# Masked copies of two batches merged over four PSUM banks, with a new order of the first four steps

## The chip, the cores and the metric

The kernel runs on one core of a Trainium2 chip. The metric is the device time of one execution in microseconds. TensorE (PE) multiplies matrices, with its weight loads shown apart (PEld); VectorE (DVE) and ScalarE (ACT) work element by element; GpSimd (POOL) and SyncE (SP) mostly issue transfers here.

## The reference

Two blocks follow each other: a gated linear attention over a state, and a two-layer network with a PReLU between its layers.

```python
# q, k, v, f_logit: (4 batches, 8 heads, 768 tokens, 48)
f = 1.0 / (1.0 + np.exp(-f_logit))
for t in range(S):
    state = f[:, :, t, :, None] * state + np.einsum('bhd,bhe->bhde', k[:, :, t], v[:, :, t])
    y[:, :, t] = np.einsum('bhd,bhde->bhe', q[:, :, t], state)

x = y.transpose(0, 2, 1, 3).reshape(3072, 384)
h = x @ w_in                                     # 384 -> 2048
g = np.maximum(h, 0.0) + alpha * np.minimum(h, 0.0)
out = g @ w_out                                  # 2048 -> 384
```

## The kernel before

The tokens of a batch are cut into 6 chunks of 128, and batches are taken in pairs (`U = 2`). That makes 12 steps: step n is a chunk `c` of a pair `bp`, `steps = [(bp, c) for c in range(NC) for bp in range(B // U)]`, so steps 0 and 1 are the first chunks of both pairs (c = 0), steps 2 and 3 the second, and so on. Each step has seven generators, whose stages end at a `yield`:

- **P** (`prepare`, 8 stages): loads q, k, f and v; sigmoid of f on ACT; products of the gates on DVE; copies of queries into the matrix `A` on ACT (L454, the last stage). It makes `qd`, `k4` and `us`, scaled queries and keys, and for c = 0 `k16` and `q16` in its fifth stage.
- **S** and **T** (`scores`, 4 stages each): the scores inside blocks of 32 tokens, S for the pair's first batch (u = 0) and T for its second (u = 1). Stage 1 is 32 small products of `k` and `qd` into PSUM (L580), stage 2 four masked copies out of PSUM into `ad` (L589, one for each lag d), stage 3 32 products of `k4` and `us` into the same banks, stage 4 masked copies again (seven of L599, or three of L615 where c = 0).
- **O** (`carry`): scores between blocks (L512), copied into `A` by ACT (L519), and the products that carry the state on (L543), added to `vs` by DVE (L553, L557). For c = 0 it has extra stages: products of `k16` and `q16` (L490), transposes (L529) and their copies by ACT (L533, one for each batch). It has 8 stages for c = 0 and 4 otherwise.
- **Y** (`attend`): ACT copies `ad` into `A` (L623, two stages of two copies), PE multiplies `A` by `vs` (L634), ACT copies the result out (L641), DVE updates `vs`, and y is transposed into `xT` by transfers, or in step 0 by products (L653).
- **K**, **M**: transposed keys for c > 0, by transfers.
- **n** (`network`): eight stages of products by `w_in` (L679), with the PReLU by ACT (L684) and DVE (L686), and then products by `w_out` (L718, or L699 in step 0).

Four single letters prepare the weights: **a**/**w** for `w_in` (ACT, then DVE L248) and **b**/**g** for `w_out`; each `a` and `b` also issues a load on SP into one of three raw buffers. **W** makes sums of `w_out`, **X** frees the banks of `more` for the network, **i** is one product of ones that nothing reads (L790), **j** 16 pairs of small ones (L798).

PSUM has eight banks of 512 f32 numbers per partition. Two tiles `pair0` and `pair1` have two banks each:

```python
pairs = [psa.tile([128, 2, 512], F32, tag=f"pair{n}", name=f"pair{n}") for n in range(2)]
```

`scores` writes `pairs[u]`; `carry` writes `off = home[0]` with L512 and `home[1]` with L490, L529 and L543; `attend` writes `pairs[0]` with L634. In step 0 `carry` and `attend` use `more` instead. The network has four further banks in turn.

The order in which PE, DVE, ACT and SP get their instructions is written out by hand as a list of stages: `START` for the first steps, then `USUAL` once a step, from step 5 on (`BEGUN = 5`). A letter with a number names the generator of that step, a letter with `+` in `USUAL` that of the next step, `n` that of the step before, and `:4` repeats. Each engine works through its own part of this list in order. POOL's order isn't written out; the scheduler sets it.

Of the kernel before, what the change touches and what calls it, by code (L numbers as in the profile page):

```python
# [8 lines left out]
F32 = mybir.dt.float32  # L9
# [3 lines left out]
I32 = mybir.dt.int32  # L13
# [5 lines left out]
DB = 32  # L19
MASKED = (1, 0)  # L20

U = 2
CH = 64
NC2 = C // CH
NB = DB // 4
# [3 lines left out]

BEGUN = 5  # L30
START = (
# [7 lines left out]
)  # L39
USUAL = "T:2 S:2 n:4 M T:2 S n P+ S n P+ n:3 Y O P+ O:2 Y O n P+ Y:2 P+ n:3 P+:3 K+"  # L40

LOOSE = ("a", "w", "b", "g", "W", "i", "j", "X")

def flat(start, usual, steps=12):
    out = []
    for word in start.split():
        key, _, times = word.partition(":")
        out += [(key,) if key in LOOSE else (key[0], int(key[1:]))] * int(times or 1)
    for n in range(BEGUN, steps + 1):
        for word in usual.split():  # L50
            key, _, times = word.partition(":")
            m = n + key.count("+") - (key == "n")
            if m < steps:
                out += [(key[0], m)] * int(times or 1)
    return out

ORDER = flat(START, USUAL)


@with_exitstack  # L60
def kernel(
# [31 lines left out]
    B, NC, _, HP, _ = qT.shape  # L93
    DM = v.shape[-1]
    H = 2 * HP
# [4 lines left out]
    T = U * C  # L100
    W = U * HP * C
# [7 lines left out]
    UW = UO.pop()  # L109
    VO = [0, 0, DB, DB + 16]  # L110
    VW = DB + 24
    QO = [0]
# [8 lines left out]
    psa = ctx.enter_context(tc.tile_pool(name="psa", bufs=1, space=bass.MemoryType.PSUM))  # L121
    early_ps = ExitStack()
    psb = early_ps.enter_context(tc.tile_pool(name="psb", bufs=1, space=bass.MemoryType.PSUM))
    pairs = [psa.tile([128, 2, 512], F32, tag=f"pair{n}", name=f"pair{n}") for n in range(2)]
    more = [psb.tile([128, 2, 512], F32, tag=f"more{n}", name=f"more{n}") for n in range(2)]
    net = {}

# [35 lines left out]
    mraw = const.tile([128, 4, NB, 4], F32, tag="mraw", name="mraw")  # L163
# [6 lines left out]
    mquad = const.tile([128, UW], F32, tag="mquad", name="mquad")  # L170
    nc.gpsimd.memset(mquad, 0.0)
    for m in range(1, NB):
        lo = UO[m] + (4 if m == 1 else 0)
        n = NB - m
        nc.gpsimd.tensor_copy(mquad[:, lo:lo + 4 * n].rearrange("p (i r) -> p i r", r=4),
                              inq[:, 0:n].unsqueeze(2).broadcast_to((128, n, 4)))
    mhalf = const.tile([128, VW], F32, tag="mhalf", name="mhalf")
    nc.gpsimd.memset(mhalf, 0.0)
    for half in range(2):
        for m in range(1, NQ):  # L180
            n = NQ - m
            lo = 16 * half + 4 if m == 1 else VO[m] + 4 * n * half
            nc.gpsimd.tensor_copy(mhalf[:, lo:lo + 4 * n].rearrange("p (i r) -> p i r", r=4),  # L183
                                  inq[:, NQ * half:NQ * half + n].unsqueeze(2).broadcast_to((128, n, 4)))
    ad = const.tile([128, U, 2, HP, DB], F32, tag="ad", name="ad")
# [76 lines left out]
    def rows(par):  # L262
        return slice(64 * par, 64 * par + D)
# [302 lines left out]
    def scores(u, bp, c, x):  # L566

        k = x["k"]


        QL, QS = (UW, UW) if c else (VW, C)
        to = pairs[u]

        def products(keys, by, lo, hi, step):
            for hp in range(HP):
                for j in range(NJ):
                    g = (u * HP + hp) * NJ + j
                    for par in range(2):
                        r_ = rows(par)
                        nc.tensor.matmul(to[DB * j:DB * (j + 1), par, hp * step + lo:hp * step + hi],  # L580
                                         lhsT=keys[r_, g * DB:(g + 1) * DB], rhs=by[r_, g, lo:hi], start=True, stop=True)

        products(k, qd, 0, QW, C)
        yield
        adu = ad[:, u].rearrange("p r h (i t) -> p (r h) i t", t=4)
        rv = to.rearrange("p r (h x) -> p (r h) x", h=HP)
        for d in range(4):
            n = 4 - d
            nc.vector.copy_predicated(  # L589
                adu[:, :, :, d:4], mraw[:, d, :, d:4].bitcast(I32).unsqueeze(1).broadcast_to((128, H, NB, n)),  # L590
                rv[:, :, QO[d]:QO[d] + NB * n].rearrange("p h (i t) -> p h i t", t=n))
        yield
        products(x["k4"], x["us"], 4, QL, QS)
        yield
        if c:
            for m in range(1, NB):
                lo = UO[m] + (4 if m == 1 else 0)
                n = DB - 4 * m
                nc.vector.copy_predicated(  # L599
                    ad[:, u, :, :, 4 * m:DB],  # L600
                    mquad[:, lo:lo + n].bitcast(I32).unsqueeze(1).unsqueeze(1).broadcast_to((128, 2, HP, n)),
                    to[:, :, 0:HP * UW].rearrange("p r (h x) -> p r h x", h=HP)[:, :, :, lo:lo + n])
        else:
            qv = to.rearrange("p r (h x) -> p (r h) x", h=HP)
            adh = ad[:, u].rearrange("p r h (a t) -> p (r h) a t", a=2)
            for m in range(1, NQ):
                n = 4 * (NQ - m)
                lo = 4 if m == 1 else VO[m]
                hi = lo + (DB - 4 if m == 1 else 2 * n)
                then, of, by = ad[:, u].rearrange("p r h t -> p (r h) t")[:, :, 4:DB], qv[:, :, lo:hi], mhalf[:, lo:hi]  # L610
                by = by.bitcast(I32).unsqueeze(1).broadcast_to((128, H, hi - lo))
                if m > 1:
                    then = adh[:, :, :, 4 * m:16]
                    of, by = (t.rearrange("p h (a t) -> p h a t", a=2) for t in (of, by))
                nc.vector.copy_predicated(then, by, of)  # L615
        yield
# [193 lines left out]
    with tc.manual_schedule(engines={mybir.EngineType.PE, mybir.EngineType.DVE, mybir.EngineType.Activation,  # L810
                                     mybir.EngineType.SP}):
        run = {}
        for n, step in enumerate(steps):
            x = {}
            for key, stage_ in zip("POYKMn", (prepare, carry, attend, keys_moved, landed, network)):
                run[key, n] = stage_(*step, x)
            run["S", n], run["T", n] = (scores(u, *step, x) for u in range(U))
        for key in ORDER:
            next(run[key] if key in run else pieces[key[0]])
# [55 lines left out]
```

## Time and profile before

| | us |
|---|---|
| median of 3 runs (lowest, highest) | 602.37 (602.04, 604.54) |
| the profiled execution | 602.81 |
| its span, first to last instruction | 601.0 |
| PE busy, PEld busy | 575.6, 516.8 |
| DVE busy (998 instructions) | 494.7 |
| ACT busy | 247.4 |
| POOL busy | 85.4 |

Busy times are sums over one engine and overlap with those of the others. L12 is line 12 of the kernel before. A PE product in f32 shows as two instructions, so 32 products are a group of x64. In a line of the timeline stand the start, the time that the group took, engine, line, operation, what is written from what, the shape, the count, and in brackets how long the engine sat idle before and what ended that. TensorE's granted clock was 0.999 over the span.

### The profile page before, as it was taken

The page shows a single profiled execution, that of the slowest core. Times are in us where ns is not written, and L with a number is a line of the kernel's source. Part 1 is how long each engine was busy: PE and PEld are TensorE (multiplying, and loading weights), DVE is VectorE, ACT ScalarE, POOL GpSimd, SP SyncE. Part 2 cuts the span into 40 slices and gives each one's busy share as a digit, 9 for nine tenths or more (in the row PEclk, how much of TensorE's full clock was granted, in tenths as well). Part 3 has the DMA queues.
Part 4 walks back from the last instruction along what each step waited for, and adds up shares of the span by engine and source line. Part 5 has one row for each costly group of instructions (what it writes and reads, how often), then busy time and mean ns, then how long its engine had stood idle before and what let it go on. Part 6 is the DMA issues. An engine that isn't in the chain of part 4 may idle for free.

```text
span 601.0 us, 18092 instructions
## 1 busy us (share of the span) xinstructions
PE 575.6 (96%) x7760; PEld 516.8 (86%) x7760; DVE 494.7 (82%) x998; ACT 247.4 (41%) x430; POOL 85.4 (14%) x162
## 2 busy tenths in 40 slices
PE   2489999999999999999999999999999999999997
PEld 1378667898899899899899899899899899899997
DVE  7989998997888779988988988988988987882351
ACT  5679952621461450550461451452343344232110
POOL 9210014013002103001200300300300300300000
PEclk9999999999999999999999999999999999999999
DMA  8778736015005302502601601601601511201000
GB/s 263 254 216 295 249 89 125 1 48 130 2 2 161 52 1 59 156 1 56 157 2 55 159 3 56 158 2 41 170 4 30 155 31 27 55 1 29 27 1 27
DMA packets 52880, 50.36 MB, mean 84 GB/s; under 512 B 26720, under 2 KB 43360, under 8 KB 52800
## 3 DMA queue, kind: packets, MB, share of 16 engines
q1 hardware_dynamic: 42784, 37.46, 21.7%
q0 software_dynamic: 5504, 9.90, 6.7%
q10 hardware_dynamic: 4512, 1.85, 1.3%
q8 instruction: 61, 1.00, 0.7%
q14 instruction: 19, 0.16, 0.1%
HBM read 36.21 MB, written 4.72 MB: 68 GB/s over the span
## 4 chain that ended last, share of the span: by engine, by line
PE 88%; DVE 7%; ACT 2%; POOL 1%; issue 1%; DMA 0%; DVEq 0%; ACTq 0%; POOLq 0%
PE ph L679 40%; PE pa L718 10%; PE pc L718 10%; PE pair L580 6%; PE pe L718 5%; PE pd L718 5%; PE pb L718 5%; PE pair L634 3%; PE pair L543 1%; DVE w_out_sb L248 1%; PE pair L512 1%; PE po L699 1%; DVE gate L686 1%; POOL mhalf L183 1%; DMA f<-in_fT 0%
## 5 line engine op out<-in xcount | busy, mean ns | idle before, releaser
L679 PE MATMUL ph<-xT,w_in_sb 128*128 128x256 f32 x1152 | 255.3, 381 | 1.4 <-DVE w_in_sb L248 1.4
L679 PEld LDWEIGHTS ph<-xT,w_in_sb 128*128 128x128 f32 x1152 | 216.9, 190 | 33.4 <-issue 2.4
L686 DVE SCALAR_TENSOR_TENSOR gate<-neg,om,ph 128x256 f32<-128x256 f32 x192 | 81.2, 476 | 33.0 <-ACT neg L684 33.0
L684 ACT ACTIVATE neg<-ph 128x512 f32<-128x512 f32 x96 | 56.1, 594 | 121.2 <-PE ph L679 101.6
L718 PE MATMUL pa<-w_out_sb,gate 128*128 128x192 f32 x352 | 62.1, 330 | 0.0
L718 PE MATMUL pc<-t,S 128*128 128x192 f32 x352 | 61.6, 328 | 0.0
L454 ACT COPY A<-q 48x512 f32<-48x512 f32 x44 | 27.1, 617 | 83.4 <-DVE q L408 82.9
L718 PEld LDWEIGHTS pa<-w_out_sb,gate 128*128 128x128 f32 x352 | 57.4, 190 | 1.3
L464 POOL DMA_DIRECT2D ksn<-kt x80 | 46.2, 586 | 85.9 <-DVE kt L422 61.3
L718 PEld LDWEIGHTS pc<-t,S 128*128 128x128 f32 x352 | 57.4, 190 | 0.4
L664 POOL DMA_DIRECT2D xT<-y x22 | 11.9, 544 | 287.5 <-ACT y L641 287.4
L599 DVE COPY_PREDICATED ad<-mquad,pair 128x224 f32<-128x224 int32 (+6 forms) x140 | 41.7, 299 | 4.1
L589 DVE COPY_PREDICATED ad<-mraw,pair 128x256 f32<-128x256 int32 (+1 forms) x96 | 41.2, 451 | 4.0 <-PE pair L580 0.8
L364 DVE TENSOR_TENSOR us<-us,fs 128x768 f32<-128x768 f32 (+5 forms) x60 | 36.9, 615 | 1.1
L765 DVE TENSOR_TENSOR S<-gate 128x512 f32<-128x512 f32 x44 | 30.3, 688 | 0.8
L718 PE MATMUL pe<-w_out_sb,S 128*128 128x192 f32 x176 | 30.6, 327 | 0.0
L718 PE MATMUL pb<-t,gate 128*128 128x192 f32 x176 | 30.4, 326 | 0.0
L718 PE MATMUL pd<-w_out_sb,S 128*128 128x192 f32 x176 | 30.4, 326 | 0.0
L623 ACT COPY A<-ad 32x512 f32<-32x512 f32 x48 | 29.4, 613 | 0.6
L641 ACT COPY y<-pair 128x512 f32<-128x512 f32 x22 | 11.8, 589 | 43.4 <-PE pair L634 43.4
L718 PEld LDWEIGHTS pe<-w_out_sb,S 128*128 128x128 f32 x176 | 28.8, 190 | 0.2
L718 PEld LDWEIGHTS pb<-t,gate 128*128 128x128 f32 x176 | 28.9, 190 | 0.0
(125 smaller groups left out, 710.6 us busy)
## 6 DMA issues: line engine op xcount, KB each, us to landing
w_out_raw<-in_w_out SPq DMA_DIRECT2D x8, 767.8 KB, 7.9
w_in_raw<-in_w_in SPq DMA_DIRECT2D x8, 767.2 KB, 9.5
out<-o SPq DMA_DIRECT2D x23, 192.0 KB, 1.9
q<-in_qT SPq DMA_DIRECT2D x8, 512.0 KB, 4.6
k<-in_kT SPq DMA_DIRECT2D x8, 512.0 KB, 7.1
f<-in_fT SPq DMA_DIRECT2D x7, 512.0 KB, 3.9
vs<-in_v SPq DMA_DIRECT2D x16, 192.0 KB
ksn<-kt SPq DMA_DIRECT2D x80, 32.0 KB, 2.2
```

Of the source, the lines that this page charges most:

```text
L364: nc.vector.tensor_tensor(us[:, :, UO[m]:UO[m] + 4 * n].rearrange("p g (i r) -> p g i r", r=4), us[:, :, skip:skip + 4 * n].rearrange("p g ...
L454: nc.scalar.copy(A[halves(cc)[1], :, par * HP:(par + 1) * HP, CH * cc:CH * (cc + 1)], q3[rows(par)].rearrange("p (u h c) s t -> p u h c (s ...
L464: (nc.gpsimd if a % 2 else nc.sync).dma_start(out=ksn[32 * b:32 * (b + 1)].rearrange("p u (h x) -> p (u h) x", h=HP)[:, :, 32 * a:32 * a + n],
L580: nc.tensor.matmul(to[DB * j:DB * (j + 1), par, hp * step + lo:hp * step + hi], lhsT=keys[r_, g * DB:(g + 1) * DB], rhs=by[r_, g, lo:hi], ...
L589: nc.vector.copy_predicated(adu[:, :, :, d:4], mraw[:, d, :, d:4].bitcast(I32).unsqueeze(1).broadcast_to((128, H, NB, n)), rv[:, :, QO[d]: ...
L599: nc.vector.copy_predicated(ad[:, u, :, :, 4 * m:DB], mquad[:, lo:lo + n].bitcast(I32).unsqueeze(1).unsqueeze(1).broadcast_to((128, 2, HP, ...
L623: nc.scalar.copy(A[s_].rearrange("p u h t -> p (u h) t")[:, :, s_], ad[s_].rearrange("p u r h t -> p (u r h) t"))
L679: nc.tensor.matmul(ph[:, j * T:(j + 1) * T], lhsT=w_in_sb[:, kt, m * 128:(m + 1) * 128], rhs=xT[:, kt], start=(kt == 0 and j == 0), stop=( ...
L684: nc.scalar.activation(neg, phv, AF.Relu, scale=-1.0)
L686: nc.vector.scalar_tensor_tensor(gate[:, m % NH, m // NH], neg[:, j], om[:, m:m + 1], phv[:, j], ALU.mult, ALU.add)
L718: nc.tensor.matmul(to[:, 0:DH], lhsT=of(f), rhs=by(f), start=(f == 0 and not more), stop=(f == NH - 1), skip_group_check=True)
L765: nc.vector.tensor_tensor(to, x_, y_, op)
```

## The change

The copies of stage 2 and stage 4 are taken out of S and made once, in T, for both batches: each instruction then reads all four banks, and there are 4 and 7 (or 3) of them for a step in place of 8 and 14 (or 6). For that the two tiles become one of four banks, with `pairs[0]` and `pairs[1]` as views of it. S's stages 2 and 4 are left empty.

```diff
-    pairs = [psa.tile([128, 2, 512], F32, tag=f"pair{n}", name=f"pair{n}") for n in range(2)]
+    four = psa.tile([128, 4, 512], F32, tag="pair", name="pair")
+    pairs = [four[:, 2 * n:2 * n + 2] for n in range(2)]
...
         products(k, qd, 0, QW, C)
         yield
-        adu = ad[:, u].rearrange("p r h (i t) -> p (r h) i t", t=4)
-        rv = to.rearrange("p r (h x) -> p (r h) x", h=HP)
-        for d in range(4):
+        for d in range(4 if u else 0):
             n = 4 - d
             nc.vector.copy_predicated(
-                adu[:, :, :, d:4], mraw[:, d, :, d:4].bitcast(I32).unsqueeze(1).broadcast_to((128, H, NB, n)),
-                rv[:, :, QO[d]:QO[d] + NB * n].rearrange("p h (i t) -> p h i t", t=n))
+                ad.rearrange("p u r h (i t) -> p (u r h) i t", t=4)[:, :, :, d:4],
+                mraw[:, d, :, d:4].bitcast(I32).unsqueeze(1).broadcast_to((128, U * H, NB, n)),
+                four.rearrange("p b (h x) -> p (b h) x", h=HP)[:, :, QO[d]:QO[d] + NB * n].rearrange("p h (i t) -> p h i t", t=n))
         yield
         products(x["k4"], x["us"], 4, QL, QS)
         yield
-        if c:
+        if not u:
+            pass
+        elif c:
             for m in range(1, NB):
                 lo = UO[m] + (4 if m == 1 else 0)
                 n = DB - 4 * m
                 nc.vector.copy_predicated(
-                    ad[:, u, :, :, 4 * m:DB],
-                    mquad[:, lo:lo + n].bitcast(I32).unsqueeze(1).unsqueeze(1).broadcast_to((128, 2, HP, n)),
-                    to[:, :, 0:HP * UW].rearrange("p r (h x) -> p r h x", h=HP)[:, :, :, lo:lo + n])
+                    ad.rearrange("p u r h t -> p (u r) h t")[:, :, :, 4 * m:DB],
+                    mquad[:, lo:lo + n].bitcast(I32).unsqueeze(1).unsqueeze(1).broadcast_to((128, 2 * U, HP, n)),
+                    four[:, :, 0:HP * UW].rearrange("p b (h x) -> p b h x", h=HP)[:, :, :, lo:lo + n])
         else:
...
```

The `else` branch (c = 0) is widened in the same way. The order of a usual step:

```diff
-USUAL = "T:2 S:2 n:4 M T:2 S n P+ S n P+ n:3 Y O P+ O:2 Y O n P+ Y:2 P+ n:3 P+:3 K+"
+USUAL = "T S T S n:4 M S T n T S P+ n P+ n:3 Y O P+ O:2 Y O n P+ Y:2 P+ n:3 P+:3 K+"
```

PE's part of it differs only in that S's second products now come before T's. `START` is new throughout; its beginning, up to where both have issued two stages of the first network, and the stretch of step 4's `carry`:

```diff
-    "i P0:4 j T0 P0:2 S0 P0 a O0:2 T0 P1 P0 O0 T0 S0 O0 P1 S0 a O0 P1 T0 S0 P1 O0:2 Y0 i P1 Y0 O0 S1 w Y0 "
-    "a Y0 X a w O1 Y0 w O1 w S1 P1 a n0 w a:2 P1 n0 ...
-    ... n3:2 M4 P4 P5 n3:2 Y4 O4:2 Y4 O4 n3 P5 n3 O4 "
+    "P0:5 a w T0 S0 P0:2 O0:2 T0 O0 T0 O0 S0 P1 a P1 S0 P1 O0 S0 T0 P0 P1 O0:2 i P1 Y0 i O1 Y0 O0 O1 Y0 w "
+    "a Y0 w a X P1 Y0 T1 S1 a:2 P1 w:2 T1 P2 a n0:2 ...
+    ... K4 T4 M4 P5 n3 S4 n3 O4 Y4:2 O4:2 n3:2 O4 ...
```

The short products `j` are dropped. Steps 1 to 4 load through POOL's queue before and after.

More of the change, by code (lines that the diff above doesn't have):

```diff
@@ L31 @@
 START = (
[7 rows of a table removed]
-)
-USUAL = "T:2 S:2 n:4 M T:2 S n P+ S n P+ n:3 Y O P+ O:2 Y O n P+ Y:2 P+ n:3 P+:3 K+"
-LOOSE = ("a", "w", "b", "g", "W", "i", "j", "X")
[7 rows of a table added]
+)
+USUAL = "T S T S n:4 M S T n T S P+ n P+ n:3 Y O P+ O:2 Y O n P+ Y:2 P+ n:3 P+:3 K+"
+LOOSE = ("a", "w", "b", "g", "W", "i", "j", "X", "e")
 def flat(start, usual, steps=12):
@@ L599, in scores @@
                 nc.vector.copy_predicated(
-                    ad[:, u, :, :, 4 * m:DB],
-                    mquad[:, lo:lo + n].bitcast(I32).unsqueeze(1).unsqueeze(1).broadcast_to((128, 2, HP, n)),
-                    to[:, :, 0:HP * UW].rearrange("p r (h x) -> p r h x", h=HP)[:, :, :, lo:lo + n])
-        else:
-            qv = to.rearrange("p r (h x) -> p (r h) x", h=HP)
-            adh = ad[:, u].rearrange("p r h (a t) -> p (r h) a t", a=2)
+                    ad.rearrange("p u r h t -> p (u r) h t")[:, :, :, 4 * m:DB],
+                    mquad[:, lo:lo + n].bitcast(I32).unsqueeze(1).unsqueeze(1).broadcast_to((128, 2 * U, HP, n)),
+                    four[:, :, 0:HP * UW].rearrange("p b (h x) -> p b h x", h=HP)[:, :, :, lo:lo + n])
+        else:
+            qv = four.rearrange("p b (h x) -> p (b h) x", h=HP)
+            adh = ad.rearrange("p u r h (a t) -> p (u r h) a t", a=2)
             for m in range(1, NQ):
@@ L609, in scores @@
                 hi = lo + (DB - 4 if m == 1 else 2 * n)
-                then, of, by = ad[:, u].rearrange("p r h t -> p (r h) t")[:, :, 4:DB], qv[:, :, lo:hi], mhalf[:, lo:hi]
-                by = by.bitcast(I32).unsqueeze(1).broadcast_to((128, H, hi - lo))
+                then, of, by = ad.rearrange("p u r h t -> p (u r h) t")[:, :, 4:DB], qv[:, :, lo:hi], mhalf[:, lo:hi]
+                by = by.bitcast(I32).unsqueeze(1).broadcast_to((128, U * H, hi - lo))
                 if m > 1:
```

12 rows, old and new, of the table START are left out of this document.

## The prediction

> **What bounds the kernel now.** I read the page's totals and chain first, then busy time by stretch, then the forms of the copies that are to be merged, then the timeline of the first 47 us and of one late step.
>
> ```profile
> span 601.0 us, 18092 instructions
> PE 575.6 (96%) x7760; PEld 516.8 (86%) x7760; DVE 494.7 (82%) x998; ACT 247.4 (41%) x430; POOL 85.4 (14%) x162
> PE 88%; DVE 7%; ACT 2%; POOL 1%; issue 1%; DMA 0%; DVEq 0%; ACTq 0%; POOLq 0%
> ...
> L684 ACT ACTIVATE neg<-ph 128x512 f32<-128x512 f32 x96 | 56.1, 594 | 121.2 <-PE ph L679 101.6
> ```
>
> TensorE (PE) is the chain for 88% of the span. Where is it idle? Busy time by stretch (us, then busy PE, PEld, DVE, ACT, POOL):
>
> ```profile
> 0.00:10.00 10.00, 2.24 (x75) 1.53 (x83) 7.92 (x11) 6.98 (x11) 9.41 (x29) 1.00 0.79 234
> 10.00:20.00 10.00, 3.69 (x244) 3.21 (x236) 8.40 (x16) 2.16 (x5) 7.09 (x15) 1.00 1.01 351
> 20.00:30.00 10.00, 5.16 (x168) 4.07 (x160) 9.59 (x25) 9.36 (x17) 1.41 (x3) 1.00 0.65 191
> 30.00:40.00 10.00, 8.34 (x323) 7.15 (x324) 8.10 (x14) 8.00 (x14) 1.93 (x3) 1.00 0.65 211
> 60.00:70.00 10.00, 8.64 (x43) 7.09 (x42) 9.93 (x19) 9.92 (x18) 0.73 (x1) 1.00 0.78 235
> 80.00:90.00 10.00, 9.75 (x211) 6.61 (x210) 9.85 (x15) 3.12 (x5) 2.29 (x4) 1.00 0.36 82
> 300.00:400.00 100.00, 100.00 (x1286) 91.58 (x1285) 88.24 (x186) 40.01 (x70) 11.41 (x20) 1.00 0.26 65
> 560.00:601.00 41.00, 37.78 (x203) 35.16 (x201) 14.12 (x30) 5.44 (x10) 0.00 (x0) 0.99 0.05 15
> ```
>
> Idle PE: 20.6 us before 40 us (7.76 + 6.31 + 4.84 + 1.66), 1.36 in 60 to 70, 0.25 in 80 to 90, 3.2 at the end. That is all 25.4 us of it. From 90 us on PE never waits, though VectorE (DVE) is nearly as full. So the change can move the time in two ways only: by idle PE before 90 us, or by new waits on PE later.
>
> **The merged copies.** Their forms now (busy, mean ns of one):
>
> ```profile
> L589 DVE COPY_PREDICATED ad<-mraw,pair 128x256 f32<-128x256 int32 x24 | 11.3, 473 | 1.6 <-PE pair L580 0.8 <-ACT ad L495 0.6
> L589 DVE COPY_PREDICATED ad<-mraw,pair 128x64 f32<-128x64 int32 x24 | 10.6, 442 | 0.8
> L599 DVE COPY_PREDICATED ad<-mquad,pair 128x224 f32<-128x224 int32 x20 | 7.9, 397 | 0.0
> L599 DVE COPY_PREDICATED ad<-mquad,pair 128x32 f32<-128x32 int32 x20 | 3.9, 194 | 0.7
> ```
>
> L599 gives (397 - 194) / (224 - 32) = 1.06 ns an element and 160 ns fixed. L589 costs the same at 64 elements as at 256: its 64 rows each cost like four elements (64 x 4 x 1.06 + 160 = 431). A merged L589 is then 160 + 2 x 271 = about 700 ns, four of them 2.8 us for 3.6 now; the seven L599 save 7 x 0.16 = 1.1. Per step DVE saves 1.8 to 1.9 us, about 21 us over the kernel (the two c = 0 steps have three second copies, not seven). Bounds: no saving (885 ns, twice 442) or, if the short rows merge better, somewhat more. I take 700, nearest to the L599 line. None of it is on PE's path after 90 us (100.00 of 100 busy), so it is costed at nothing there.
>
> **The new order of steps 0 to 3.** The path that lets PE start the network of step 0:
>
> ```profile
> 20.52 1.25 ACT L454 COPY A<-q 48x512 f32<-48x512 f32 x2 [2.57 <-DVE q L408]
> 21.67 1.48 ACT L519 COPY A<-more 32x256 f32<-32x256 f32 x4
> ...
> 29.65 1.07 ACT L533 COPY ksn<-more 128x512 f32<-128x512 f32 x2
> 30.61 2.51 ACT L623 COPY A<-ad 32x512 f32<-32x512 f32 x4
> 30.78 1.53 PE L543 MATMUL more<-vs,ksn 64*48 64x48 f32 x64 [3.45 <-ACT ksn L533]
> ...
> 32.24 1.22 PE L790 MATMUL more<-ones 128*128 128x256 f32 x2
> 33.39 1.34 PE L580 MATMUL pair<-qd,k 48*32 48x80 f32 x64
> 34.66 2.97 PE L634 MATMUL more<-A,vs 128*64 128x64 f32 x64
> 34.90 1.05 DVE L248 TENSOR_TENSOR w_in_sb<-w_in_sb,w_in_lead 128x768 int16<-128x768 int16 x1
> ...
> 37.56 1.58 PE L490 MATMUL pair<-us 48*32 48x16 f32 x128
> 38.62 1.12 DVE L557 TENSOR_TENSOR vs<-vs,more 48x384 f32<-48x384 f32 x2
> 39.89 2.83 PE L653 MATMUL xt<-y,dense 128*128 128x256 f32 x12 [0.75 <-DVE vs L557]
> 42.55 2.75 PE L679 MATMUL ph<-xT,w_in_sb 128*128 128x256 f32 x12
> ```
>
> 1. ACT works in order. P0's last stage (L454) stood before L519, where ACT was waiting; now it stands behind P1's second stage and in front of P1's fourth and of L533: + 1.15 (its start to L519's). The first `w` (L248) is put ahead of P0's scans on DVE: they move by 1 us, but L519 waited for L454 anyway, so only 0.2 gets through. L533's products (L543) start at about 30.78 + 1.35 = 32.1 and end at 33.6.
> 2. Then PE had L790, S1's first products (L580) and Y0's products (L634, at 34.66). Now it has L790 twice (2 x 1.15), O1's first products (L490, 1.58), and L634: 33.6 + 2.3 + 1.6 = 37.5, 2.85 later. P1's fifth stage, on which L490 waits, comes at about 35.8 when I add up DVE's instructions behind P1's sigmoid (an estimate); L790 hides it, and later than 35.9 it adds one for one.
> 3. L653 follows 5.2 behind L634's start, by way of DVE's L553 and L557: 42.7. L490 covered that stretch and no longer does.
> 4. T1's and S1's first products now stand before the network: 42.7 + 2.7 + 1.3 = 46.7 for the first L679, against 42.55. T1's 0.65 of it is work that came later before, so the new idle time is 4.15 - 0.65 = 3.5.
> 5. Later waits of PE can be won back:
>
> ```profile
> PE ph L679 <- DVE w_in_sb L248: 1.4, 1, 1.4
> PE pair L580 <- DVE vs L557: 0.2, 1, 0.2
> ```
>
> PE comes 3.5 later and DVE has less to do, so I take both as gone: - 1.6. The next late thing is the same `vs` at S2's first products: adding up DVE's instructions in the new order I find it 0.25 ahead of PE, so if DVE is later than I think (merged copies at 885 ns, three sets of four by then, about 2 us) PE waits up to 2. T3's first copies, too, now come behind a scan pair and one more gate, before O2's L543; about 0.5 of cover stays. Both at nothing. The four loads of steps 1 to 4 go by POOL's queue before and after, POOL's memsets stay at P's fourth stage; the loads of the weights keep their order on SP and their three raw buffers: nothing. Sum of the order: 3.5 - 1.6 = + 1.9, between 0 (idle at the start as before, 1.6 won back, less what 1. overstates) and + 5.5 (nothing won back, DVE 2 late).
>
> Beside these rows: L634's 64 instructions took 2.97 at 34.66 and 2.08 in the late step quoted below, at a granted clock of 1.00 both times. The Trainium skill, "TensorE: Matmul & The Clock Gate", Part 1 (the HAM clock gate), says the array runs at half clock until it has been busy for some 3.4 us. By that rule L634 would now follow over 5 us of PE work and take about 2.1: 0.9 off the sum, which I don't take.
>
> **One tile of four banks.** `pair0` and `pair1` were tiles of their own; now both are views of `four`. Waits are set between an instruction that writes a tile and one that reads it. By piece or by tile? On SBUF by piece: L718's first products start before the gates are all written.
>
> ```profile
> 119.71 1.65 DVE L686 SCALAR_TENSOR_TENSOR gate<-neg,om,ph 128x256 f32<-128x256 f32 x4
> ...
> 120.25 2.87 PE L718 MATMUL pa<-w_out_sb,gate 128*128 128x192 f32 x16
> ```
>
> In PSUM it looks otherwise. L533 is two copies, one for each batch and bank; L543's first products need batch 0 alone and write bank 0, but start at 30.78, after both (29.65 + 1.07 = 30.72), with PE idle. And in a late step:
>
> ```profile
> 309.98 0.70 PE L512 MATMUL pair<-q,kh 48*64 48x64 f32 x32
> 310.50 0.90 PE L543 MATMUL pair<-vs,kt 64*48 64x48 f32 x64
> 310.75 1.49 ACT L519 COPY A<-pair 32x256 f32<-32x256 f32 x4 [1.80 <-PE pair L512]
> ...
> 316.73 2.08 PE L634 MATMUL pair<-A,vs 128*64 128x64 f32 x64
> ...
> 318.86 1.07 ACT L641 COPY y<-pair 128x512 f32<-128x512 f32 x2 [3.17 <-PE pair L634]
> ```
>
> L641's first copy reads the bank of batch 0, which is full halfway through L634 (317.8), yet ACT waits, idle, until all 64 are done (318.81). So a reader waits for the whole tile's writer, and a writer for the whole tile's readers. In the steps of `USUAL`, O's L512 writes `pairs[0]`, ACT's L519 reads it, and PE goes straight on with L543 into `pairs[1]`. With one tile, L543 waits for L519's end: 310.75 + 1.49 = 312.24, and 0.06 more, as at 30.78, in place of 310.68 (L512's end): 1.62 us of idle PE, with the whole network queued behind it. Seven steps (5 to 11): 11.3. Step 4 is worse: the order there is n3 O4 Y4 Y4 O4 O4, so ACT does the gate's L684 (0.59, some 0.2 behind PE), four L623 (2.5) and L519 (1.49) before L543 may start, with only L512 (0.7) for cover: 0.2 + 0.6 + 2.5 + 1.5 + 0.1 - 0.7 = 4.2; with the overlap of starts 4.0. Steps 1 to 3 have network work between O's second and third stage: nothing. Sum of the tie: 15.3; bounds 0 (waits by bank) and about 18 (a second place of 0.4 a step).
>
> **Sum.** 601.0 + 1.9 + 15.3 = 618.2 span. The profiled execution took 602.81, 1.81 over its span and 0.44 over the median 602.37; on the median: 602.37 + 17.2 = **619.6**.
>
> **Rivals.**
> - *Waits by bank.* Then L543 goes on at 310.68 as now, the tie costs nothing, and 602.37 + 1.9 = 604.3 is left, between 602 and 608. For it: the evidence above is of tiles of two banks, none of four. Against: both rows show the whole tile. This is also what the Trainium skill, "PSUM — Partial Sum Buffer", section on bank collisions, asks for: a guard by bank and quadrant. By that rule the time is 604.3; the trace speaks against it, since its waits are wider.
> - *Faster: DVE is the bound before 90 us.* The chain is 7% DVE, all before 90 us, and it holds the copies of steps 0 to 2. If the start isn't late and the merged copies shorten that chain by 1.2 + 1.2 + 0.7, the time is 599.3. It decides only if the idle 20.6 shrinks; more than 1.6 behind it there isn't to win. Against: ACT and L634's place, not DVE, set the first network product.
> - *The merge saves nothing* (885 ns a copy) and waits go by bank: DVE is 2 us late at S2: 606.3.
>
> **Chances.** Tie 0.63 (own range 613 to 625); by bank 0.27; faster 0.06; no saving 0.04. Half a per cent, 3.0 us, is what a measurement here can tell. Slower by more: 0.63 + 0.04 + 0.09 of the by-bank case (over 605.4) = 0.76. Within: 0.17. Faster: 0.06 + 0.01 = 0.07. The range for 8 in 10 starts inside the by-bank case and ends with the tie's bound: 602.5 to 625.
>
> **What would show it.** Tie: from step 4 on PE is idle before L543 with ACT's L519 as releaser, 1.6 a step, and L543 starts after L519 ends. By bank: L543 starts at L512's end. Order: first L679 at about 46.7, the 1.4 wait on L248 gone. Copies: L589 near 700 ns, L599 from 230 to 630. The prediction is wrong if L543 overlaps L519, or if the first L679 comes before 43.

## The result and the profile after

| | before | after |
|---|---|---|
| median on one chip (4 runs each) | 603.31 us | 627.04 us (624.98 to 628.08) |
| ratio, 95% interval | | 1.040 [1.036, 1.043] |
| profiled execution, its span | 602.81, 601.0 | 627.64, 625.8 |
| PE busy, PE idle in the span | 575.6, 25.4 | 580.3, 45.5 |
| DVE busy | 494.7 | 481.2 |

The change costs 4.0%. The forecast was 619.6 in a range of 602.5 to 625, and the measured time lies 2.0 above that range. The sign and the waits came as forecast, the cost did not: 17.2 over the kernel before were forecast, 23.7 were measured. (The forecast started from a median of 602.37, of three runs; with the fourth it is 603.31.) Line numbers of the changed kernel differ by one or two: L543, L519, L512, L589, L599, L679, L718 are now L544, L520, L513, L588, L601, L681, L720. In the experiments they can shift by one more.

The head of the page after, with the row of the granted clock and the engines of the chain:

```profile
span 625.8 us, 17876 instructions
...
PE 580.3 (93%) x7728; PEld 520.8 (83%) x7728; DVE 481.2 (77%) x874; ACT 248.9 (40%) x430; POOL 85.5 (14%) x162
...
PEclk9999999999999899999999989999999999998999
...
PE 63%; ACT 2%; issue 0%; DVE 0%
```

DVE has 13.5 us less to do and the program is 24.8 longer. PE has 20.1 more of idle time, and is itself busy 4.7 longer though it has 32 instructions fewer (the short products `j`); three digits of the clock's row are 8, where before all were 9. Three of PE's waits in the changed kernel that are new and one that is longer (total, times, longest, us):

```profile
PE pair L544 <- ACT A L520: 15.2, 8, 4.0
...
PE xt L655 <- DVE vs L558: 2.3, 1, 2.3
PE pe L720 <- issue: 0.8, 1, 0.8
PE pair L544 <- DVE ad L588: 0.5, 1, 0.5
```

The first row is the tie, by which L544 stands until ACT has read the other half of the tile: eight waits, one in each of steps 4 to 11, 15.2 in all. The wait of 1.4 on the weights (L248, now L249) is gone. One late step by time:

```profile
272.26 0.69 PE L513 MATMUL pair<-q,kh 48*64 48x64 f32 x32
...
273.03 1.49 ACT L520 COPY A<-pair 32x256 f32<-32x256 f32 x4 [1.80 <-PE pair L513]
...
274.57 0.94 PE L544 MATMUL pair<-vs,kt 64*48 64x48 f32 x64 [1.61 <-ACT A L520]
...
275.43 2.87 PE L720 MATMUL pc<-t,S 128*128 128x192 f32 x16
```

L544 starts 0.05 after ACT's four copies end (273.03 + 1.49 = 274.52), though its products go to the other half of the tile; the network's L720 stands behind it. In step 4 there is more than idle:

```profile
210.94 0.69 PE L513 MATMUL pair<-q,kh 48*64 48x64 f32 x32
215.62 1.53 PE L544 MATMUL pair<-vs,kt 64*48 64x48 f32 x64 [3.99 <-ACT A L520]
217.08 5.21 PE L681 MATMUL ph<-xT,w_in_sb 128*128 128x256 f32 x12
```

The 64 products of L544 take 1.53 in place of 0.94, and 12 products of L681 take 5.21, where the same 12 take 2.86 elsewhere. The windows of that place, and of one of the later waits (L544 at 370.98), show why; the number behind POOL's is the granted clock:

```profile
215.62:217.62 2.00, 2.00 (x65) 1.87 (x66) 0.00 (x0) 0.00 (x0) 0.00 (x0) 0.50 0.00 0
217.62:219.62 2.00, 2.00 (x6) 1.59 (x5) 0.00 (x0) 0.00 (x0) 0.00 (x0) 0.50 0.00 0
219.62:221.62 2.00, 2.00 (x6) 1.55 (x6) 0.00 (x0) 0.00 (x0) 0.00 (x0) 0.50 0.00 0
221.62:223.62 2.00, 2.00 (x13) 1.91 (x12) 0.61 (x2) 0.60 (x1) 0.00 (x0) 0.93 0.00 0
370.98:372.98 2.00, 2.00 (x68) 1.95 (x69) 1.97 (x4) 1.96 (x4) 0.00 (x0) 0.77 0.00 0
372.98:374.98 2.00, 2.00 (x8) 2.00 (x7) 1.32 (x3) 1.38 (x3) 0.00 (x0) 0.50 0.00 0
374.98:376.98 2.00, 2.00 (x12) 2.00 (x12) 0.55 (x2) 0.00 (x0) 0.00 (x0) 0.87 0.00 0
```

Behind the idle 4.0 of step 4 PE ran at half clock for a little over 6 us: (3 x 0.50 + 0.07) x 2 = 3.1 lost. Behind the idle 1.6 at 370.98, and again at 565.57, the clock dipped for about 3.4 us: (0.23 + 0.50 + 0.13) x 2 = 1.7 each. The other five waits of 1.6 had no dip. Together 6.6 us that are no wait: they hide in the durations of products that nobody waits for.

### The profile page after: what moved, and what is told of

Read it like the earlier page. It is cut to its first block, busy times and chain, and to the rows that moved or that the text cites. A ratio compares the mean times of both kernels' runs of the same rounds, so it can differ in the third digit from the quotient of the medians.

```text
span 625.8 us, 17876 instructions
## 1 busy us (share of the span) xinstructions
PE 580.3 (93%) x7728; PEld 520.8 (83%) x7728; DVE 481.2 (77%) x874; ACT 248.9 (40%) x430; POOL 85.5 (14%) x162
## 4 chain that ended last, share of the span: by engine, by line
PE 63%; ACT 2%; issue 0%; DVE 0%
PE ph L681 28%; PE pc L720 8%; PE pa L720 8%; PE pe L720 4%; PE pd L720 4%; PE pb L720 4%; PE pair L581 4%; PE pair L636 3%; ACT A L520 2%; PE pair L544 1%; PE pair L513 1%; DVE o L724 0%
## 5 line engine op out<-in xcount | busy, mean ns | idle before, releaser
L681 PE MATMUL ph<-xT,w_in_sb 128*128 128x256 f32 x1152 | 258.3, 384 | 0.0
L681 PEld LDWEIGHTS ph<-xT,w_in_sb 128*128 128x128 f32 x1152 | 218.3, 191 | 32.3 <-issue 1.4
L720 PE MATMUL pc<-t,S 128*128 128x192 f32 x352 | 64.9, 340 | 0.0
L720 PE MATMUL pa<-w_out_sb,gate 128*128 128x192 f32 x352 | 61.9, 329 | 0.0
L720 PEld LDWEIGHTS pc<-t,S 128*128 128x128 f32 x352 | 60.8, 199 | 0.4
L720 PEld LDWEIGHTS pa<-w_out_sb,gate 128*128 128x128 f32 x352 | 57.5, 190 | 1.3
L588 DVE COPY_PREDICATED ad<-mraw,pair 128x512 f32<-128x512 int32 (+3 forms) x48 | 35.1, 731 | 1.3
L601 DVE COPY_PREDICATED ad<-mquad,pair 128x448 f32<-128x448 int32 (+6 forms) x70 | 30.8, 440 | 2.4 <-PE pair L581 0.3
L554 DVE TENSOR_TENSOR vs<-vs,f 48x768 f32<-48x768 f32 x20 | 19.1, 953 | 17.3 <-PE pair L636 14.8
L720 PE MATMUL pe<-w_out_sb,S 128*128 128x192 f32 x176 | 30.8, 327 | 0.8 <-issue 0.8
L720 PE MATMUL pb<-t,gate 128*128 128x192 f32 x176 | 30.4, 326 | 0.0
L720 PE MATMUL pd<-w_out_sb,S 128*128 128x192 f32 x176 | 30.4, 326 | 0.0
L720 PEld LDWEIGHTS pe<-w_out_sb,S 128*128 128x128 f32 x176 | 28.9, 190 | 1.2 <-issue 1.1
```

The source lines that it names most:

```text
L588: nc.vector.copy_predicated(ad.rearrange("p u r h (i t) -> p (u r h) i t", t=4)[:, :, :, d:4], mraw[:, d, :, d:4].bitcast(I32).unsqueeze(1 ...
L601: nc.vector.copy_predicated(ad.rearrange("p u r h t -> p (u r) h t")[:, :, :, 4 * m:DB], mquad[:, lo:lo + n].bitcast(I32).unsqueeze(1).uns ...
L681: nc.tensor.matmul(ph[:, j * T:(j + 1) * T], lhsT=w_in_sb[:, kt, m * 128:(m + 1) * 128], rhs=xT[:, kt], start=(kt == 0 and j == 0), stop=( ...
L720: nc.tensor.matmul(to[:, 0:DH], lhsT=of(f), rhs=by(f), start=(f == 0 and not more), stop=(f == NH - 1), skip_group_check=True)
```

## The experiments

The theory: one tile makes L544 wait for L520 (the tie), that is the idle time, and an idle that is long enough costs a spell of half clock behind it. Rivals: the merged copies cost something themselves; the new order of the first steps does; the waits are as predicted and what is missing lies elsewhere.

**e1 and e2: the tile and the copies taken apart.** Both keep the changed order. In e1 the two tiles are back, in e2 the one tile stays, and in both T's stages copy each batch by itself.

```diff
e1: +    pairs = [psa.tile([128, 2, 512], F32, tag=f"pair{n}", name=f"pair{n}") for n in range(2)]
e1, e2:
-        for d in range(4 if u else 0):
+        for b, to_ in enumerate(pairs if u else []):
+            for d in range(4):
...
```

> The order of the changed kernel, but two PSUM tiles again and the copies once for each batch, as before (both batches' copies in T's stages). Theory (the single tile makes L543's products wait for ACT's reads of the other pair, and PE's idle time pulls its clock down): those waits go, the clock is 0.99 or more, the time is 603 to 606. Rival (the new order costs it): 620 or more. Rival (the merged instruction costs it): 603 to 606 as well; the next kernel tells them apart.

> The same as the kernel with two tiles and separate copies, but the two pairs are views of one tile of four banks. Theory (single tile): 8 waits of PE for ACT's A copies of 15 us together, clock down as in the changed kernel, 625 to 630, since DVE's extra 14 to 20 us lie beside PE. Rival (the merged instructions or their wait for both batches cost it): 603 to 606. Rival (waits by bank): 603 to 606.

e1: 610.17 (608.84 to 610.81), ratio 1.010 [1.007, 1.014], span 607.1. e2: 632.51 (627.48 to 634.22), ratio 1.046 [1.040, 1.052], span 625.7. PE's waits for `pair` behind L543 or L544, first of e1, then of e2:

```profile
PE pair L543 <- DVE ad L590: 2.7, 1, 2.7
```
```profile
PE pair L544 <- ACT A L520: 14.6, 8, 3.3
...
PE pair L544 <- DVE ad L591: 2.1, 1, 2.1
```

The only difference between the two is the tile, and with it come the wait on L520 (14.6 in e2, none in e1) and 18.6 us of span. The merged copies aren't what costs. They even save a little: without them T3's copies end 2.7 (e1) or 2.1 (e2) late for the carry's products of step 2, with them 0.5 (the row L588 above). e1 lies above the 603 to 606 that were expected. Its late steps take 46.39 each, as in the kernel before; its 6.1 over the span before lie in the first steps (first network products at 48.55 in place of 42.55, the products of `xt` in 4.51 in place of 2.83) and in that 2.7. e2's profiled execution lies in the expected 625 to 630, its median above.

**e3: step 4's idle made short.** Only the place of Y4's copies changes, so that ACT has no more than the gate and L520 between L513 and L544.

```diff
-    ... n3 O4 Y4:2 O4:2 n3:2 O4 ...
+    ... n3 O4:2 Y4:2 O4 n3:2 O4 ...
```

> The changed kernel with one move in the list: in step 4, the ACT copies of O's second stage stand ahead of Y's two stages of copies, so PE's longest idle time, 4.0 us, should become about 1.7. Theory (idle time, then 7 us at half clock): 2.3 less idle and 3 to 3.5 less by the clock, 5 to 6 in all: 621 to 622, granted clock 0.99 or more. Rival (the clock's dip has nothing to do with the idle time): 2.3 less, 624.7, the clock as it was.

620.67 (619.39 to 621.83), ratio 1.027 [1.022, 1.032].

```profile
PE pair L544 <- ACT A L520: 12.9, 8, 1.6
```
```profile
214.53:216.53 2.00, 2.00 (x69) 1.84 (x70) 0.07 (x1) 1.96 (x4) 0.00 (x0) 1.00 0.00 0
216.53:218.53 2.00, 2.00 (x11) 1.79 (x11) 0.00 (x0) 0.66 (x2) 0.00 (x0) 1.00 0.00 0
```

2.3 us less of idle, and the loss against the kernel before, each on its own chip, is 18.2 in place of 23.7: 5.5 less. Step 4's wait is now 1.6 and PE's clock behind it stayed at 1.00, so its 3.1 went with it: 2.3 + 3.1 = 5.4. The two traces agree: step 5's L544 comes 4.04 sooner (270.53, against 274.57), though e3's first L544 had come 1.41 later (33.61, against 32.20), 5.45 together.

**e4: work put between L513 and L544.** The order alone covers L520, with the tile and the merged copies as they are.

```diff
-USUAL = "... n P+ n:3 Y O P+ O:2 Y O n P+ ..."
+USUAL = "... n P+ n:2 O:2 n Y P+ O Y O n P+ ..."
-    ... n3 O4 Y4:2 O4:2 n3:2 O4 ...
+    ... n3 O4:2 Y4:2 n3 O4 n3 O4 ...
```

> The changed kernel, still one tile and merged copies, with network products put between O's second and third stage: in USUAL, O's first two stages stand ahead of the ninth network stage (5.2 us of PE work), in step 4 ahead of the eighth. Theory: ACT's reads are over when L543's products come up, the 15 us of waits go, the clock stays up, 603 to 605. Rival (one tile causes other waits that take their place, or the order of steps 0 to 3 costs more than 2 us): 607 or more.

608.42 (607.8 to 610.06), ratio 1.009 [1.006, 1.011], span 606.7, no wait on L520 left. The loss is 6.0 in place of 23.7: 17.7 come back by order alone. The waits and the dips went as the theory said, but the time is above its 603 to 605 and in the rival's range: 3.4 are there before the seven late steps (step 5's second scores start at 249.44, before at 246.05). What stays in the late steps is seen in PE's timeline:

```profile
261.79 0.69 PE L513 MATMUL pair<-q,kh 48*64 48x64 f32 x32
262.41 2.87 PE L720 MATMUL pa<-w_out_sb,gate 128*128 128x192 f32 x16
...
267.81 0.94 PE L544 MATMUL pair<-vs,kt 64*48 64x48 f32 x64
268.68 2.87 PE L720 MATMUL pc<-t,S 128*128 128x192 f32 x16
```

L513 and L544 now stand apart among the 128 x 128 products, and that has a price: a step of e4 takes 46.73 (237.35 to 284.08), one of the kernel before 46.39: 0.34 more, or 0.17 for each of the two groups.

**e5: the idle doubled.** ACT's four copies of L520 are issued twice (no change in what is computed).

```diff
+                for _ in range(2 if c else 1):
                     nc.scalar.copy(A[s_]..., of...)
```

> The changed kernel with ACT's four carry copies (L520) of every step but the first two issued twice, to the same place with the same values: 1.4 to 1.5 us more of idle PE in front of L544 in each of the seven steps 5 to 11 and in step 4, some 11.5 us in all. Theory (the idle costs its own length and, once it is long enough, a spell of half clock behind it): the idle of 3.1 us now trips the clock in most steps, not in two of seven; each dip of some 6 us at 0.5 costs about 3 more: 645 to 658, granted clock below 0.975. Rival (only the idle itself counts, the clock's dips are an accident of one run): 627 + 11.5 = 638 to 640, clock as before at 0.988.

650.02 (648.62 to 650.15), ratio 1.078 [1.076, 1.080], clock 0.968. Its wait, and the windows behind the L545 of step 5, where the wait was 3.18:

```profile
PE pair L545 <- ACT A L521: 27.9, 8, 5.6
```
```profile
280.53:282.53 2.00, 2.00 (x66) 1.91 (x67) 1.06 (x2) 1.96 (x4) 0.00 (x0) 0.55 0.00 0
282.53:284.53 2.00, 2.00 (x9) 2.00 (x8) 0.62 (x2) 1.35 (x3) 0.00 (x0) 0.59 0.03 8
284.53:286.53 2.00, 2.00 (x15) 2.00 (x14) 0.65 (x2) 0.00 (x0) 0.00 (x0) 1.00 0.00 0
```

All seven waits of 3.2 were followed by half clock; here it costs (0.45 + 0.41) x 2 = 1.7, in the other six 1.6 to 1.7. The 12.7 of added idle would have made 640; the time is 650, and the rival, that only the idle counts, is out by 10. In the traces the dips behind these eight waits make 7.9 of that (14.4 in place of 6.5), and the first network products, which come 2.0 later (47.88, against 45.88), about the rest.

**e6: the reader taken out of the tile.** Tile, merged copies and first steps as changed, but from step 2 on L513 writes two banks of the network's ring, and O's first three stages stand together.

```diff
-        off = home[0]
+        off = [bank(f"off{p}_{i}") for p in range(2)] if c else [home[0][:, p] for p in range(2)]
...
-USUAL = "... n P+ n:3 Y O P+ O:2 Y O n P+ ..."
+USUAL = "... n P+ n:2 O:3 n Y P+ Y O n P+ ..."
```

> The changed kernel with the four-bank tile, the merged copies and its order of the first steps, but the carry's products L513 go into two banks of the network's ring (one for each parity) and not into the tile, so that L544 has no reader of the tile to wait for; the three carry stages O.1 to O.3 stand next to each other in the usual steps, and ACT does eight copies half as long in place of four. Theory (the tie through L520 and the clock dips that follow it make the whole loss): no wait of L544 on L520 is left, granted clock 0.995 or more, 602 to 607. Rival (the one tile or the merged copies cost PE in some other way too): 610 or more, with a new releaser in front of PE. A third way: two more banks a step in a ring of four make the network's products wait for ACT, some 0.5 a step: 607 to 612.

609.45 (607.78 to 612.02), ratio 1.012 [1.008, 1.015], span 606.1, clock 0.997. No wait on L520. It is above what the theory gave, for the third reason, but in one place and not in each step:

```profile
105.03 4.51 PE L681 MATMUL ph<-xT,w_in_sb 128*128 128x256 f32 x12 [3.29 <-DVE gate L688]
109.47 1.86 PE L581 MATMUL pair<-us,k 48*32 48x112 f32 x128
```

In step 2 DVE is late with the gates, the two extra banks leave the network two fewer, PE waits 3.29, and the clock dips again (12 products in 4.51 in place of 2.86). e9, which takes the banks only from step 4 on, has no such wait.

**e7: the start put back in part.** On e6, the first lines of `START` are arranged more like the old ones (`i` first, T1 and S1 sooner), and T3's copies come one stage earlier. (In that place they overwrite part of step 2's scores before ACT has copied them, so half of step 2's attention has step 3's values; the work is the same.)

```diff
-    "P0:5 a w T0 S0 P0:2 O0:2 T0 O0 T0 O0 S0 P1 a P1 S0 P1 O0 S0 T0 P0 P1 O0:2 i P1 Y0 i ...
+    "i P0:5 a T0 S0 P0:3 O0:2 T0 w O0 T0 O0 S0 P1:2 a S0 P1 O0 S0 T0 P1 O0:2 i P1 Y0 O1 ...
-    ... S3 T3 Y2 n1 T3 n1:2 ...
+    ... S3 T3:2 Y2 n1:3 ...
```

> As the kernel with the carry in banks of its own, with the first products of the start in the old place of the first line (less of step 1's preparation ahead of them) and T3's copies one stage earlier than L544 of step 2. Theory (what is left over the kernel before is the start's order): 1 to 3 us under that kernel, 599 to 604, first network products before 45, no wait on L588. Rival (the start depends on when the loads land and on the clock of L655, not on this order): within 1 us of it.

609.56 (607.67 to 612.99), ratio 1.011 [1.008, 1.013]: nothing gained where 599 to 604 were expected, the rival's answer. The first network products start at 45.83, against 45.80 in e6. The wait of L655 fell from 2.25 to 0.17, but the first scores wait 4.5 for the merged copies (2.7 in e6), and a wait of 1.9 on ACT is new. So moving stages shifted the waits of the start from one place to another and left its end where it was.

**e8: the old order with one tile.** The kernel before, its copies and its order; only the two tiles become views of one.

```diff
-    pairs = [psa.tile([128, 2, 512], F32, tag=f"pair{n}", name=f"pair{n}") for n in range(2)]
+    four = psa.tile([128, 4, 512], F32, tag="pair", name="pair")
+    pairs = [four[:, 2 * n:2 * n + 2] for n in range(2)]
```

> The kernel before with one thing changed: both batches' score tiles are views of one tile of four banks; copies and order as they were. Theory (a product into any part of the tile waits for every reader of it): batch 1's products stand behind batch 0's copies on DVE, which start some 8 us after batch 0's products and last 1.8 and 2.3, and L543 behind L519: some 12 to 14 of idle PE a step, 700 to 760 with the clock's dips; the new order of products and copies is then not a choice but what makes the one tile bearable. Rival (waits go by bank): 602 to 604, no new wait.

769.54 (one run), span 767.7: 9.5 above the 700 to 760 that were expected, because a late step waits 8.95 + 5.48 + 1.61 = 16.0 where 12 to 14 were priced. The waits of PE, and one step by time:

```profile
PE pair L581 <- DVE ad L590: 65.0, 9, 8.9
PE pair L581 <- DVE ad L600: 41.2, 8, 5.5
PE pair L544 <- ACT A L520: 15.7, 9, 2.9
```
```profile
384.32 0.92 PE L581 MATMUL pair<-qd,k 48*32 48x80 f32 x64
...
392.28 1.85 DVE L590 COPY_PREDICATED ad<-mraw,pair 128x256 f32<-128x256 int32 x4
394.19 1.34 PE L581 MATMUL pair<-qd,k 48*32 48x80 f32 x64 [8.95 <-DVE ad L590]
```

In this order T's products come first, then T's copies, then S's products. S's products go to banks that nobody reads, and still stand 8.95 until T's copies are done: the tie has nothing to do with ACT, O or the merged copies. 122 us of waiting are the price of the one tile where the order isn't made for it. So the new place of S's and T's stages belongs to the change; L513 and L544 are the one place of a usual step where the order still has a reader between two writers.

**e9: e6 without its wait.** The carry has banks of its own only from step 4 on.

```diff
-        off = ... if c else [home[0][:, p] for p in range(2)]
+        off = ... if steps.index((bp, c)) >= 4 else [home[0][:, p] for p in range(2)]
```

> The changed kernel with its four-bank tile, merged copies and first steps as they are; from step 4 on the carry's products go into two banks of the network's ring, as in e6, and O.1 to O.3 stand together; steps 1 to 3 keep the tile (in e6 the two banks taken there put 3.3 of idle and a dip of the clock into step 2). Theory: e6's span of 606.1 less the 4.7 by which its step 3 was later than in the changed kernel, 601.4, so 602.5 to 605.5, and nothing left of 24.7: the merged copies by themselves neither cost nor gain more than 0.5%. If the 13 us less DVE work were worth anything it would come below 601; if the order of the first steps cost more than the 2.7 I read from the trace, above 606.

605.97 (604.2 to 607.77), ratio 1.006 [1.003, 1.008], span 602.4, clock 1.0. The median lies 0.5 above the expected 602.5 to 605.5, the profiled execution (604.2, the lowest of seven) inside. The second score products of steps 5 and 6, first in the kernel before, then in e9:

```profile
246.05 1.86 PE L580 MATMUL pair<-us,k 48*32 48x112 f32 x128
292.44 1.86 PE L580 MATMUL pair<-us,k 48*32 48x112 f32 x128
```
```profile
247.47 1.86 PE L581 MATMUL pair<-us,k 48*32 48x112 f32 x128
293.86 1.86 PE L581 MATMUL pair<-us,k 48*32 48x112 f32 x128
```

The step is 46.39 in both: without the tie the merged copies leave the late steps as they were, to 0.01 us. What is left in these two traces is 1.42, brought along from the first steps. On the medians it is 3.3: e9's three runs with a granted clock of 1.000 have spans of 602.4 to 602.8, its four runs with 0.994 to 0.997 of 604.2 to 606.0, and a mean of 0.997 over 605 is 1.8 us lost, about one dip. Of all the versions with the change in it this is the fastest, and it is still not faster than the kernel before: DVE's 13 us are worth nothing where PE is full.

## Why the prediction was wrong: the waits were right, their price was not

*Step 1, the copies.* This held. The widths came as forecast: L601 from 230 to 643 ns (forecast 230 to 630), L588 near 730 ns (forecast 700).

```profile
L588 DVE COPY_PREDICATED ad<-mraw,pair 128x128 f32<-128x128 int32 x12 | 8.8, 730 | 0.4
L588 DVE COPY_PREDICATED ad<-mraw,pair 128x512 f32<-128x512 int32 x12 | 8.7, 726 | 0.1
L601 DVE COPY_PREDICATED ad<-mquad,pair 128x64 f32<-128x64 int32 x10 | 2.3, 230 | 0.3
```

The three groups of copies fell by 18.0 (86.7 to 68.7) where about 21 were forecast, and DVE's busy time in all by 13.5; where the difference between these two lies wasn't traced. It is off the path, as said: e9's late step is unchanged.

*Step 2, the order of the first steps.* This held too: L544 of step 0 came at 32.20 (forecast 32.1), L636 at 37.04 (37.5), L655 at 41.60 (42.7), the first L681 at 45.88 (46.7), and the wait on the weights is gone.

```profile
32.20 1.53 PE L544 MATMUL more<-vs,ksn 64*48 64x48 f32 x64 [4.05 <-ACT ksn L534]
...
37.04 2.31 PE L636 MATMUL more<-A,vs 128*64 128x64 f32 x64
41.60 2.83 PE L655 MATMUL xt<-y,dense 128*128 128x256 f32 x12 [2.26 <-DVE vs L558]
...
45.88 8.04 PE L681 MATMUL ph<-xT,w_in_sb 128*128 128x256 f32 x36
```

Of the forecast +1.9 there remain 1.4 at step 5, by e9. The tie of T3's copies with the L544 of step 2, costed at nothing, came to 0.5. L636's 64 products took 2.31; the sum had kept 2.97 for them and left the 2.1 aside. The 1.4 is for a start without a dip: behind the idle of 2.26 in front of L655 the clock stayed up in the changed kernel, e3 and e9, and dipped in e1, e4 and e5, which cost 1.6 to 1.7.

*Step 3, the tie.* The waits held: 15.3 were forecast and 15.2 measured, in the same eight places, 1.61 in each usual step (forecast 1.62) and 3.99 in step 4 (4.0). e2 against e1 and e8 against the kernel before show the mechanism. The rival by bank is refuted: in e8 products into other banks wait 8.95. So is the rival by which the merge saves nothing (730 ns a copy, not 885). The Trainium skill, "PSUM — Partial Sum Buffer", section on bank collisions, says what must be guarded, by bank and quadrant; this program's waits are wider, the whole tile, as the rows of the kernel before had it.

*The sum: this is the step that failed.* It priced an idle PE at the length of the idle, and took the products around it at their old durations: two terms stood at nothing without a reason. What the trace and e9 show, in span:

| term | forecast | measured |
|---|---|---|
| order of the first steps | 1.9 | 1.4 |
| tie, idle time | 15.3 | 15.2 |
| half clock behind the idle | none | 3.1 + 2 x 1.7 = 6.6 |
| L513 and L544 no longer in a row | none | 7 x 0.2 = 1.5 |
| sum | 17.2 | 24.7 (of 24.8) |

The fourth row: a step without a dip takes 48.21 (290.84 to 339.05), 1.82 more than before, of which 1.61 is idle; the rest is 0.2, a cost of the kind that e4 shows, 0.34 a step there. e3 and e5 bear out the third row from both sides: a shorter idle in step 4 gives back more than its length, a doubled one takes more than its length in every step. The Trainium skill, "TensorE: Matmul & The Clock Gate", Part 1, has this mechanism: half clock after an idle window of some 3.4 us, and again full after some 3.4 us of work, the windows running freely. The forecast used it only to ask whether one stage of the start gets faster. Put to the tie, a window at half clock would have been an estimate of 1.7 for each dip, and 1.72 is what the rows above give for the two short dips; the dip of step 4 cost 3.1. That PE must stand idle for 3.4 isn't borne out, since the clock dipped behind two idles of 1.6.

The range ended at 625 because its upper bound held only more idle ("a second place of 0.4 a step"), no slower PE.

## What to carry to other kernels

Before two PSUM tiles are made one, list every place where one engine reads a part of it and another writes a different part, because in a program like this one each can become a wait: here 122 us with the old order, 15 with the new. Price an idle PE at its length and the half clock that may follow (here 1.6 to 3.1 for each dip in the late steps of the changed order), and cover it with work, or take the reader out of the tile; e4 and e9 won back 18 and 20 of the 24 us so. And shorter work on an engine that isn't the bound gained nothing here, so it couldn't pay for a wait on the one that is.

## What the hardware showed that was not expected

- A dip doesn't follow the idle's length smoothly. Of the idles of 1.6 in front of L544, 2 of 7 were followed by one in the changed kernel, none of 7 in e2, 1 of 8 in e3, 3 of 8 in e8; of two idles of 2.8 and 2.9 in e8, one; of the idles of 3.2 in e5, 7 of 7; of those of 5.5 to 8.9 in e8, all. A dip behind 1.6 or 3.2 lasted 3.1 to 3.4 us, one behind 4 us or more between 3.8 and 6.3. Behind the idles of 1.6 the clock fell not at once but some 0.9 us after the idle's end in all six cases, about when L544's 64 small products (0.94) were through. Whether those small products count as idle for the clock, and why one idle of 1.6 is followed by a dip and the next isn't, no run tells. e2's runs differ by 6.7 among themselves, and the clock alone doesn't make that: one with 0.994 took 632.19, the profiled one with 0.995 took 627.48.
- The clock's column can't be trusted in the first 35 us. The 64 products of L544 at 32 us took 1.53 (0.94 later) in both the changed kernel and e5; the column says 1.00 in the one and 0.50 in the other. There the durations show the half clock and the column doesn't.
- A masked copy in many short pieces costs by pieces: L588 takes 730 ns for 128 elements a partition as for 512, where L601 moves 128 in 300.
